# Attention products of stacked head pairs as four 64x64 tiles side by side

## The chip, the core and the metric

The kernel runs on one core of a Trainium2 chip. The metric is the device time of one execution in microseconds (us). A core has several engines that work side by side, each through its own instructions in order: TensorE (PE in the profile; PEld is its loading of weights), VectorE (DVE), ScalarE (ACT), GpSimd (POOL) and SyncE (SP). On this kernel POOL and SP also issue the DMA transfers. TensorE takes a stationary operand (the weights) and streams the columns of a second operand past it; the results go to PSUM, which has eight banks of 512 32-bit columns on 128 partitions.

## The reference

Two parts follow each other: an attention with a local and a pooled half, and a gated feed-forward network. The sizes are 8 batches, 8 heads, 576 positions, 64 channels a head; 4608 tokens of 512 channels, and 1536 hidden channels.

```python
q_d, k_d, v_d = (x.reshape(B, H, S // 4, 4, D).mean(axis=3) for x in (q, k, v))
out_up = np.repeat(sm_attn(q_d, k_d, v_d), 4, axis=2)      # softmax attention on 144 pooled positions
mask = np.abs(pos[:, None] - pos[None, :]) < 4             # local: keys at a distance of up to 3
scores = np.where(mask, scale * q @ k.T, -1e9)
attn = softmax(scores)
x = (out_up + attn @ v).transpose(0, 2, 1, 3).reshape(B * S, H * D)
out = (np.maximum(x @ w_gate, 0) * (x @ w_val)) @ w_out
```

## The kernel before

**The work and its order.** The 64 heads are worked on as 32 pairs, numbered from 0. Four pairs make one batch's share of the feed-forward input `xT`; the tokens then go through the feed-forward network in nine chunks of 512. The attention of later pairs is laid between the feed-forward work of earlier chunks. There is no loop that sets this order: the long string `SEQ` is a list of some 2,300 steps, emitted one after another, and every engine takes its own instructions in that order. A step such as `exp/a0/1@4` names the kind (`exp`), the pair within its chunk (`a` or `b`, and the half `1` of chunk `4`), and an argument (`0`). The kinds that matter here:

- `qk`, `v`, `v4`: DMA loads of a pair's Q and K, of its V, and of V for pooling. `qk` and `v` are issued by POOL, `v4` of the later pairs by SP. The step `scores` also issues the transposing DMA of the pair three further on, on SP.
- `pool` (DVE), `kk` and `kd` (ACT, L805 and L812), `scores` (PE, L842 and L846), `exp` (ACT, L855), `ed` (ACT, L860), `mask` (DVE, L868): from Q and K to the exponentials of the local and of the pooled scores.
- `o` (PE, L873, L888, L893): the denominators and numerators of the softmax.
- `ln` and `inv` (ACT, L905 and L923): one over the denominator, as Exp(-Ln(den)). `xn` (DVE, L908) multiplies, `xsum` (DVE, L912) adds the two halves into `xT`.
- `sq`, `up`, `p`, `q`, `qv` (PE, L1289, L1193, L1030): the 256-column products of the feed-forward network, which is computed in seven products for eight on 2x2 blocks; `sk`, `uk` (ACT, L1300) copy a quarter of a PSUM bank onto another so that PE adds to it; `sf`, `uf` (ACT, L1305, or DVE, L1307) give the finished quarters; `vh`, `hg`, `hv` (PE, L945) are plain 512-column products; `gt` (DVE, L1384) multiplies gate and value.

**The pairs that the change touches.** The pairs from 12 on (`NEW = 12`, 20 pairs) are stacked: the keys of head 0 stand on partitions 0 to 63 and those of head 1 on 64 to 127. A block of 58 queries sees 64 keys, so the local half is ten blocks; the pooled half is three sets of 48 keys. The weights of every product are 128x128 and block-diagonal, with zeros between the heads, and one matmul serves both heads. For one pair the step `o` comes in four parts, which `SEQ` places singly:

- `o/?00` (`emit_pooled`, L870, twice): three matmuls of 144 columns with a constant into the denominators, and three with the pooled V into the numerators;
- `o/?01`: the local denominators, two matmuls of 290 and 286 columns with `one_st`;
- `o/?10` and `o/?11`: the local numerators, five blocks of 58 columns each, with the block's V as weights.

The denominators lie in PSUM banks 4 and 5 and the numerators in 6 and 7, each as 576 local and 144 pooled columns, with head 0 on partitions 0 to 63. One `ln` over 128 partitions then reads all 720 denominators. The same banks hold scores and feed-forward quarters at other times.

**The earlier pairs** (below 12) are not stacked. They use two tiles of 64 weight columns beside each other, one for a head (L751, L760, L772, L781).

Of the kernel before, what the change touches and what calls it, by code (L numbers as in the profile page):

```python
# [11 lines left out]
AF = mybir.ActivationFunctionType  # L12
# [53 lines left out]
sq/4.0.0.1/0@2 hv/5/1@1 gate/5/1@1 xq/1/0@2 gate/4/1@1 xq/2/0@2 scores/a/0@2 sumhi/0/0@2 xq/3/0@2 v2/a/0@2 next/0/1@1
sumhi/1/0@2 next/1/1@1 sq/4.0.0.5/0@2 zero/k/1 kk/b1/0@2 vh/10.6/0@2 sk/4.0.0.1/0@2 sq/4.0.0.2/0@2 sq/4.0.0.6/0@2
exp/a0/0@2 sk/4.0.0.2/0@2 up/2.1/0@2 sq/4.0.0.7/0@2 sq/4.0.0.3/0@2 uk/2.1/0@2 sf/4.0.0.11/0@2 sk/4.0.0.5/0@2
vh/4.7/0@2 mask/a0/0@2 up/2.5/0@2 ed/a/0@2 kk/b0/0@2 sf/4.0.0.22/0@2 sq/4.0.0.4/0@2 up/2.6/0@2 sf/4.0.0.12/0@2
gt/4.7.0/0@2 sum/2/0@2 o/a00/0@2 sf/4.0.0.21/0@2 kd/b1/0@2 sq/0.0.2.1/0@2 sq/0.0.2.5/0@2 o/a01/0@2 o/a11/0@2  # L70
uk/2.2/0@2 uk/2.5/0@2 kd/b0/0@2 sk/0.0.2.1/0@2 sk/0.0.2.5/0@2 sum/3/0@2 up/2.7/0@2 zero/v/2 gt/10.6.1/0@2 next/0/0@2
v1/a/0@2 after/3/0@2 uf/2.22/0@2 ln/a0/0@2 inv/a/0@2 up/2.3/0@2 sq/0.0.2.6/0@2 o/a10/0@2 sq/0.0.2.2/0@2 sk/0.0.2.2/0@2
up/2.2/0@2 sq/0.0.2.3/0@2 sq/0.0.2.7/0@2 xn/a0/0@2 sf/0.0.2.11/0@2 uf/2.11/0@2 sf/0.0.2.22/0@2 sf/0.0.2.12/0@2
pool/a/0@2 up/2.4/0@2 uf/2.21/0@2 v2/b/0@2 uf/2.12/0@2 scores/b/0@2 exp/b0/0@2 v4/b/0@2 v1/b/0@2 sq/1.1.0.1/0@2
sq/1.1.0.5/0@2 sq/0.0.2.4/0@2 vh/0.7/0@2 sk/1.1.0.1/0@2 sk/1.1.0.5/0@2 ed/b/0@2 sf/0.0.2.21/0@2 sq/1.1.0.6/0@2
sq/1.1.0.2/0@2 vh/6.3/0@2 sk/1.1.0.2/0@2 sf/1.1.0.11/0@2 kk/a0/0@2 kd/a1/0@2 gt/0.7.2/0@2 sq/1.1.0.7/0@2
sq/1.1.0.3/0@2 vh/1.0/0@2 sf/1.1.0.22/0@2 sf/1.1.0.12/0@2 mask/b0/0@2 v4/a/0@2 kd/a0/0@2 kk/a1/0@2 sq/2.2.0.1/1@2
sq/1.1.0.4/0@2 sq/2.2.0.5/1@2 sf/1.1.0.21/0@2 gt/6.3.3/0@2 sk/2.2.0.1/1@2 o/b00/0@2 o/b01/0@2 gt/1.0.0/0@2 xsum/a/0@2
o/b10/0@2 o/b11/0@2 vh/7.1/0@2 next/2/0@2 gt/7.1.1/0@2 sq/2.2.0.6/1@2 up/0.1/1@2 ln/b0/0@2 inv/b/0@2 xn/b0/0@2
scores/a/1@2 sk/2.2.0.5/1@2 sk/2.2.0.2/1@2 uk/0.1/1@2 exp/a0/1@2 ed/a/1@2 kk/b1/1@2 sq/2.2.0.7/1@2 sq/2.2.0.2/1@2  # L80
sq/2.2.0.3/1@2 qk/a1/1@2 v1/a/1@2 up/0.5/1@2 sf/2.2.0.22/1@2 tm/b/0@2 sq/2.2.0.4/1@2 vh/8.7/1@2 qk/b3/1@2 v/a/1@2
next/1/0@2 v2/b/1@2 qk/a0/1@2 qk/a2/1@2 qk/a1/0@3 mask/a0/1@2 pool/b/1@2 sf/2.2.0.11/1@2 sf/2.2.0.21/1@2
sf/2.2.0.12/1@2 gt/8.7.1/1@2 up/0.6/1@2 kk/a0/1@2 sq/3.2.1.1/1@2 sq/3.2.1.5/1@2 kd/b0/1@2 uk/0.2/1@2 sk/3.2.1.1/1@2
vh/2.4/1@2 o/a10/1@2 uk/0.5/1@2 sq/3.2.1.6/1@2 sk/3.2.1.5/1@2 sk/3.2.1.2/1@2 qk/a3/1@2 gt/2.4.0/1@2 xsum/b/0@2
o/a00/1@2 up/0.7/1@2 kk/b0/1@2 sq/3.2.1.7/1@2 sf/3.2.1.22/1@2 next/3/0@2 uf/0.22/1@2 tm/a/1@2 kd/b1/1@2 v/b/1@2
pool/a/1@2 sq/3.2.1.2/1@2 o/a01/1@2 ln/a0/1@2 inv/a/1@2 sq/3.2.1.3/1@2 o/a11/1@2 sq/3.2.1.4/1@2 up/0.2/1@2
sf/3.2.1.21/1@2 scores/b/1@2 exp/b0/1@2 xn/a0/1@2 v/b/0@3 mask/b0/1@2 xsum/a/1@2 ed/b/1@2 up/0.4/1@2 uf/0.21/1@2
sf/3.2.1.11/1@2 up/0.3/1@2 sq/5.2.0.1/1@2 sq/5.2.0.5/1@2 o/b00/1@2 o/b01/1@2 vh/3.0/1@2 sk/5.2.0.1/1@2 uf/0.11/1@2
uf/0.12/1@2 kd/a0/1@2 sq/5.2.0.6/1@2 sf/3.2.1.12/1@2 gt/3.0.1/1@2 sk/5.2.0.2/1@2 o/b10/1@2 vh/9.1/1@2 gt/9.1.2/1@2
sk/5.2.0.5/1@2 ln/b0/1@2 sq/5.2.0.3/1@2 sq/5.2.0.2/1@2 sq/5.2.0.7/1@2 o/b11/1@2 v4/b/0@6 kd/a1/1@6 v2/b/1@6  # L90
sf/5.2.0.12/1@2 inv/b/1@2 sf/5.2.0.22/1@2 pool/a/1@6 v2/a/1@6 qk/b3/0@7 kd/a1/1@2 vh/5.4/1@2 sf/5.2.0.11/1@2
sq/5.2.0.4/1@2 sf/5.2.0.21/1@2 kk/a1/1@2 xn/b0/1@2 vh/11.1/1@2 gt/5.4.0/1@2 up/2.1/0@3 tm/b/1@2 v2/a/1@2 qk/b1/1@2
qk/b2/1@2 v1/b/1@2 qk/a0/0@3 qk/a2/0@3 v4/b/1@2 qk/b0/1@2 gt/11.1.1/1@2 qk/b3/0@3 qk/a3/0@3 qk/b0/0@3 v4/a/1@2
qk/b2/0@3 v/a/0@3 sq/4.0.0.1/0@3 kk/b0/0@3 sk/4.0.0.1/0@3 kk/b1/0@3 xsum/b/1@2 qk/b1/0@3 xq/0/0@3 xq/1/0@3 xq/2/0@3
scores/a/0@3 uk/2.1/0@3 vh/10.6/0@3 qk/b0/1@6 qk/a1/0@7 qk/a3/1@6 sq/4.0.0.2/0@3 sq/4.0.0.5/0@3 sq/4.0.0.6/0@3
sf/4.0.0.11/0@3 sumhi/0/0@3 xq/3/0@3 sk/4.0.0.5/0@3 sk/4.0.0.2/0@3 vh/4.7/0@3 v2/a/0@3 next/0/1@2 sumhi/1/0@3
next/1/1@2 sq/4.0.0.7/0@3 ed/a/0@3 exp/a0/0@3 kk/a1/0@3 sq/4.0.0.3/0@3 sf/4.0.0.22/0@3 up/2.5/0@3 sq/4.0.0.4/0@3
sf/4.0.0.21/0@3 up/2.6/0@3 uk/2.5/0@3 uk/2.2/0@3 sf/4.0.0.12/0@3 gt/4.7.0/0@3 o/a00/0@3 sq/0.0.2.1/0@3 sq/0.0.2.5/0@3
mask/a0/0@3 sum/2/0@3 sum/3/0@3 gt/10.6.1/0@3 pool/b/0@3 o/a01/0@3 o/a11/0@3 up/2.7/0@3 sk/0.0.2.1/0@3 sk/0.0.2.5/0@3
sq/0.0.2.6/0@3 sk/0.0.2.2/0@3 up/2.3/0@3 ln/a0/0@3 inv/a/0@3 kd/b1/0@3 sq/0.0.2.3/0@3 sq/0.0.2.2/0@3 sq/0.0.2.7/0@3  # L100
up/2.2/0@3 o/a10/0@3 uf/2.22/0@3 sf/0.0.2.12/0@3 uf/2.11/0@3 kd/b0/0@3 next/0/0@3 up/2.4/0@3 v1/a/0@3 after/3/0@3
sq/1.1.0.1/0@3 sf/0.0.2.22/0@3 xn/a0/0@3 sq/0.0.2.4/0@3 sk/1.1.0.1/0@3 uf/2.21/0@3 v2/b/0@3 uf/2.12/0@3 scores/b/0@3
# [207 lines left out]
def kernel(  # L310
# [559 lines left out]
    def emit_pooled(hp, lo, weights):  # L870
        for w in range(3):
            e = ep[hp % 2].rearrange("p (c t) -> p c t", c=2)
            nc.tensor.matmul(  # L873
# [744 lines left out]
```

## Time and profile before

| | |
|---|---|
| three runs | 334.12, 335.16, 335.21 us (median 335.16) |
| span of the profiled execution | 333.2 us, 9166 instructions |
| PE, DVE, ACT, POOL busy | 327.2, 288.9, 268.4, 185.2 us |
| granted TensorE clock | 1.000 |
| loads and stores | 43.96 MB by DMA |

The profile is of one execution. Its span runs from the program's first to its last instruction; the time of that same execution, which has some more around it, is not marked among the three. In rows of groups the columns are: line, engine, operation, out<-in by the program's names, shapes, count, then busy us and mean ns of one, then idle time before them and what ended it. A matmul's shape `128*128 128x256` means weights of 128 rows by 128 columns and 256 streamed columns. Durations of matmuls contain the time from the first column to the last result, so consecutive ones overlap in the list.

### The profile page before, as it was taken

How to read it: one execution, taken by the hardware profiler on the slowest of the kernel's cores; microseconds unless marked ns; L12 is line 12 of the kernel's file. 1: busy time of each engine (PE TensorE's matmuls, PEld its weight loads, DVE VectorE, ACT ScalarE, POOL GpSimd, SP SyncE). 2: the span in 40 equal slices, each digit the busy share in tenths (PEclk: the TensorE clock that was granted, in tenths of full speed). 3: DMA queues.
4: the chain of work that ended last, by engine and by line, in shares of the span. 5: the costliest groups of instructions: out<-in, count | busy, mean ns of one | idle time of the engine just before them, and what ended most of it. 6: DMA issues, size and time to landing. Idle time of an engine off the chain costs nothing.

```text
span 333.2 us, 9166 instructions
## 1 busy us (share of the span) xinstructions
PE 327.2 (98%) x3456; PEld 243.8 (73%) x3456; DVE 288.9 (87%) x574; ACT 268.4 (81%) x649; POOL 185.2 (56%) x268
## 2 busy tenths in 40 slices
PE   7999999999999999999999999999999999999996
PEld 3876556666577787778687868786878678888875
DVE  6795779999998989999999989979998998788792
ACT  4968887789988989899789989898889548787852
POOL 8974855938979889767968997855420000000000
PEclk9999999999999999999999999999999999999999
DMA  9999999999999999999999999999200102003014
GB/s 147 174 185 213 173 199 172 143 182 143 151 182 147 221 114 189 160 210 87 215 148 187 118 206 156 200 95 198 41 31 3 65 0 97 1 18 111 2 56 135
DMA packets 155264, 43.96 MB, mean 132 GB/s; under 512 B 140012, under 2 KB 149908, under 8 KB 155220
## 3 DMA queue, kind: packets, MB, share of 16 engines
q0 software_dynamic: 116800, 19.51, 82.6%
q1 hardware_dynamic: 38308, 23.83, 34.2%
q8 instruction: 27, 0.44, 0.6%
q14 instruction: 17, 0.14, 0.2%
q10 hardware_dynamic: 112, 0.04, 0.1%
HBM read 46.63 MB, written 9.44 MB: 168 GB/s over the span
## 4 chain that ended last, share of the span: by engine, by line
PE 91%; DMA 4%; POOL 1%; ACT 1%; DVE 1%; issue 1%; SPq 1%; POOLq 0%; ACTq 0%
PE ps L945 28%; PE ps L1289 26%; PE ps L1193 18%; PE ps L1030 3%; PE ps L873 2%; DMA v<-in_v_dram 2%; DMA qk<-in_q_dram 2%; PE ps L893 2%; PE ps L846 2%; PE ps L888 1%; PE ps L553 1%; PE ps L842 1%; PE ps L631 1%; PE ps L661 1%; PE ps L650 1%
## 5 line engine op out<-in xcount | busy, mean ns | idle before, releaser
L945 PE MATMUL ps<-xT,wv_sb 128*128 128x512 f16 x352 | 89.9, 379 | 0.0
L945 PEld LDWEIGHTS <-wv_sb 128*128 128x128 f16 x352 | 32.7, 98 | 26.0
L1384 DVE SCALAR_TENSOR_TENSOR gT<-r,ps 128x512 f16<-128x512 f16 x55 | 37.3, 681 | 4.8 <-PE ps L945 4.0
L1289 PE MATMUL ps<-xT,qk 128*128 128x256 f16 x240 | 41.3, 272 | 0.1
L472 POOL DMA_DIRECT2D qk<-in_q_dram x46 | 34.1, 741 | 10.6 <-DMA qkT<-qk 6.1
L472 POOL DMA_DIRECT2D qk<-in_k_dram x46 | 33.6, 733 | 11.4 <-issue 6.5
L1300 ACT COPY ps<-ps 128x256 f32<-128x256 f32 x80 | 28.6, 365 | 6.3 <-PE ps L1289 5.0
L1289 PE MATMUL ps<-xT,wg_sb 128*128 128x256 f16 x180 | 33.6, 272 | 0.0
L490 POOL DMA_DIRECT2D vw<-in_v_dram x40 | 28.9, 730 | 6.9 <-DMA qk<-in_q_dram 4.6
L540 DVE TENSOR_REDUCE qkd<-qkT 128x288 f16<-128x1152 f16 x23 | 30.8, 1340 | 0.0
L1204 ACT COPY ps<-ps 128x256 f32<-128x256 f32 x54 | 19.7, 370 | 12.7 <-PE ps L1193 11.4
L1289 PEld LDWEIGHTS <-qk 128*128 128x128 f16 x240 | 22.4, 97 | 7.6 <-issue 0.7
L610 POOL TENSOR_TENSOR vd<-v 48x192 f16<-48x192 f32 x40 | 25.7, 642 | 1.7
L945 PE MATMUL ps<-xT,wg_sb 128*128 128x512 f16 x104 | 26.6, 379 | 0.0
L1305 ACT CAST r<-ps 128x256 f16<-128x256 f32 x55 | 20.0, 372 | 7.5 <-PE ps L1289 6.6
L602 POOL TENSOR_TENSOR v<-v 112x384 f32<-112x384 f32 (+1 forms) x21 | 21.5, 1024 | 7.6 <-DMA v<-in_v_dram 7.3
L1289 PEld LDWEIGHTS <-xo 128*128 128x128 f16 x240 | 22.7, 98 | 3.4 <-DVE xo L1024 0.2
L1289 PE MATMUL ps<-wt,xo 128*128 128x256 f16 x180 | 24.4, 272 | 0.0
L923 ACT ACTIVATE rden<-rden 128x720 f32<-128x720 f32 x28 | 22.5, 804 | 0.7
L957 DVE TENSOR_TENSOR gT<-r,ps 128x512 f16<-128x512 f16 x24 | 16.2, 680 | 6.8 <-ACT r L954 4.0
L1289 PEld LDWEIGHTS <-wg_sb 128*128 128x128 f16 x180 | 16.4, 98 | 6.1 <-issue 0.2
L1307 DVE TENSOR_TENSOR r<-ps,xT 128x256 f16<-128x256 f32 x44 | 17.3, 418 | 3.4 <-PE ps L1289 2.4
(181 smaller groups left out, 876.3 us busy)
## 6 DMA issues: line engine op xcount, KB each, us to landing
out_dram<-y_sb SPq DMA_DIRECT2D x24, 256.0 KB, 4.2
v<-in_v_dram SPq DMA_DIRECT2D x20, 192.0 KB, 5.3
qk<-in_q_dram POOLq DMA_DIRECT2D x46, 72.0 KB, 6.1
qk<-in_k_dram POOLq DMA_DIRECT2D x46, 72.0 KB, 6.0
vw<-in_v_dram POOLq DMA_DIRECT2D x38, 80.0 KB, 5.1
v<-in_v_dram SPq DMA_DIRECT2D x20, 144.0 KB, 5.9
out_dram<-y_sb SPq DMA_DIRECT2D x22, 128.0 KB, 1.8
vw<-in_v_dram POOLq DMA_DIRECT2D x12, 168.0 KB, 6.9
```

Of the source, the lines that this page charges most:

```text
L472: nc.gpsimd.dma_start(dst.rearrange("p (j h d) -> p j h d", h=2, d=64)[:, :, hh, :], _dap(src, off + hh * S * D, [[D, 96], [NQ * D, NB], [ ...
L490: nc.gpsimd.dma_start(t[lo : lo + 64, j0:j1, lo : lo + 64], _dap(v, base + j0 * QB * D, [[D, 64], [QB * D, j1 - j0], [1, D]]),)
L540: nc.vector.tensor_reduce(out=qkd[hp % 2].rearrange("p i t -> p (i t)"), in_=qkT[hp % 4][:, 0 : 2 * S].rearrange("p (t f) -> p t f", f=4), ...
L602: nc.gpsimd.tensor_tensor(out=m, in0=t[:, :, 0:128], in1=t[:, :, 128:256], op=ALU.add)
L610: nc.gpsimd.tensor_tensor(out=vp[hp % 3][lo : lo + 48, :, lo : lo + 64], in0=m[:, :, 0:64], in1=m[:, :, 64:128], op=ALU.add)
L923: nc.scalar.activation(out=rden, in_=rden, func=AF.Exp, scale=-1.0)
L945: nc.tensor.matmul(out=out, lhsT=w[:, kk, bass.ts(jj, 128)], rhs=xT[:, kk, c * TCH : (c + 1) * TCH], start=(kk == 0), stop=(kk == 3),)
L1193: nc.tensor.matmul(out=out, lhsT=self.left[i][t], rhs=self.right[i][t], start=(i == 1 and t == 0), stop=(t == n - 1), skip_group_check=True,)
L1289: nc.tensor.matmul(out=out, lhsT=self.left[i - 1][k], rhs=self.right[i - 1][k], start=(i == 1 and k == 0), stop=(k == n - 1), skip_group_c ...
L1300: nc.scalar.copy(out=o, in_=x)
L1305: nc.scalar.copy(out=o, in_=self.d if i == 11 else self.a)
L1384: lambda c, jj, b, t: nc.vector.scalar_tensor_tensor(out=gT[c % 2][:, jj, :], in0=tg[t], scalar=0.0, in1=ps[:, b, :], op0=ALU.max, op1=ALU ...
```

## The change

The four parts of `o` of a stacked pair become one step, `emit_quads`. It uses only the diagonal quarters of the old weights. Each head has one stream of numerators (ten local blocks, three pooled matmuls) and one of denominators (two local, three pooled). Head 0 takes partitions 0 to 63 of the operands, and head 1 64 to 127. The numerators go to the head's own partitions, and the denominators to those of the other head, so that the four streams work on four different quarters of TensorE's array. Head 0 takes the local blocks first, and head 1 the pooled ones, then the blocks of the second bank and then those of the first. `emit_tiles` lists the matmuls of all four streams by a planned start (a step of 30 ns at least, else columns / 2.4 + 3; 4 ns between the streams).

Since the denominators stand on the other head's partitions, `ln` is split in two instructions of 64 partitions, which bring them back. `inv`, `xn` and `xsum` stay.

`SEQ` has a new order. It is the same for its first 457 steps; from there on it holds the same steps except for `o` (one for four) and `ln` (two for one), in other places: the loads `qk`, `v` and `v4` too.

```diff
+    def emit_tiles(streams):
+        steps = []
+        for n, stream in enumerate(streams):
+            t = 4.0 * n
+            for step in stream:
+                steps.append((t, n, step))
+                t += max(30, step[2].free_size() / 2.4 + 3)
+        for _, _, (out, left, right, first, last) in sorted(steps, key=lambda x: x[:2]):
+            nc.tensor.matmul(out=out, lhsT=left, rhs=right, start=first, stop=last, skip_group_check=True)
+
-    def emit_out_st(hp, i):
+    def emit_quads(hp):
         num, den = 512 * 6, 512 * 4
...
+        e, s, r = ep[hp % 2].rearrange("p (c t) -> p c t", c=2), es[hp % 2], hp % 3
+
+        streams = []
+        for h in range(2):
+            p, o = 64 * h, 64 - 64 * h
+            rows, some = slice(p, p + 64), slice(p, p + 48)
+            nums = [
+                (flat[rows, num + 222 + a : num + 222 + a + n], vb[hp % NL][rows, j, rows], s[rows, a : a + n], True, True)
+                for j, (a, n) in enumerate(blocks())
+            ]
+            dens = [
+                (flat[o : o + 64, den + 222 + a : den + 222 + b], one_st[rows, rows], s[rows, a:b], True, True)
+                for a, b in ((0, 290), (290, S))
             ]
+            pool = [
+                [
+                    (flat[t : t + 64, n + 798 : n + 942], left(w), e[some, :, SD:] if w == 2 else e[some, w, 0:SD],
+                     w == 0, w == 2)
+                    for w in range(3)
+                ]
+                for t, n, left in (
+                    (p, num, lambda w: vp[r][some, w, rows]),
+                    (o, den, lambda w: four_st[some, rows]),
                 )
+            ]
+            for a, b, k in ((nums, pool[0], 5), (dens, pool[1], 1)):
+                streams.append(a + b if h == 0 else b + a[k:] + a[:k])
+        emit_tiles(streams)
...
-    def emit_ln_st():
-        nc.scalar.activation(out=rden_st, in_=flat[:, 2048 + 222 : 2048 + 942], func=AF.Ln)
+    def emit_ln_st(h):
+        p, o = 64 * h, 64 - 64 * h
+        nc.scalar.activation(out=rden_st[p : p + 64], in_=flat[o : o + 64, 2048 + 222 : 2048 + 942], func=AF.Ln)
...
-        "o": lambda hp, a: emit_out_st(hp, 2 * int(a[0]) + int(a[1])),
-        "ln": lambda hp, a: emit_ln_st(),
+        "o": lambda hp, a: emit_quads(hp),
+        "ln": lambda hp, a: emit_ln_st(int(a)),
```

More of the change, by code (lines that the diff above doesn't have):

```diff
@@ L68 @@
[L68 to L72, printed above, removed]
@@ L98 @@
[L98 to L102, printed above, removed]
```

347 lines of the change are left out of this document (164 added, 183 removed).

## The prediction

> **What bounds the kernel now.** I read the page's busy shares and its chain of waits first, then a table of busy time by stage, then who waited for whom inside the stage that the change touches.
>
> ```profile
> span 333.2 us, 9166 instructions
> PE 327.2 (98%) x3456; PEld 243.8 (73%) x3456; DVE 288.9 (87%) x574; ACT 268.4 (81%) x649; POOL 185.2 (56%) x268
> PEclk9999999999999999999999999999999999999999
> PE 91%; DMA 4%; POOL 1%; ACT 1%; DVE 1%; issue 1%; SPq 1%; POOLq 0%; ACTq 0%
> ```
>
> PE is busy almost throughout at its full granted clock, and 91% of the chain is PE. The stacked pairs (the 20 pairs numbered 12 to 31) have their products between 98.5 and 264.5 us, so that is the stage to read. The table by stage gives busy us, and the count of instructions, of each engine:
>
> ```profile
> core 0: us, PE busy (x) PEld busy (x) DVE busy (x) ACT busy (x) POOL busy (x), PEclk, DMA share, GB/s
> 98.50:264.50 166.00, 165.60 (x1668) 127.38 (x1667) 153.19 (x277) 145.97 (x347) 113.47 (x169) 1.00 1.27 141
> 264.50:333.20 68.70, 65.48 (x573) 55.68 (x570) 54.08 (x122) 43.49 (x138) 0.00 (x0) 1.00 0.16 51
> 151.00:158.50 7.50, 7.50 (x92) 6.45 (x91) 7.01 (x13) 7.42 (x18) 5.20 (x10) 1.00 1.56 81
> 140.00:150.00 10.00, 10.00 (x96) 7.46 (x95) 9.33 (x15) 9.54 (x24) 7.06 (x11) 1.00 1.06 201
> ```
>
> In the 166.0 us of that stage PE works 165.6, DVE 153.2 and ACT 146.0. ACT idles 20.0 us. The lists of waits of this stage (us in total, times, longest) say why:
>
> ```profile
> ACT r L1305 <- PE ps L1289: 6.6, 12, 1.0
> ACT ps L1300 <- PE ps L1289: 4.7, 13, 0.8
> PE ps L873 <- POOL vd L610: 0.4, 1, 0.4
> ```
>
> ACT waits for PE; PE waits for nobody but once, 0.4 us. So PE sets the pace alone, and a PE microsecond saved is a microsecond gained only as long as ACT and DVE, at 88% and 92%, can follow.
>
> **Part 1: the products as 64x64 tiles.** A matmul's listed duration contains its latency, so I price one by the distance to the next start. PE's timeline (start, us, line, operands, count) around the products of pair 12 in the kernel before:
>
> ```profile
> 98.65 0.35 PE L873 MATMUL ps<-att 128*128 128x144 f16 x3
> 98.83 0.35 PE L873 MATMUL ps<-att,vd 128*128 128x144 f16 x3
> 99.02 0.38 PE L1289 MATMUL ps<-xT,wg_sb 128*128 128x256 f16 x2
> ...
> 99.46 0.41 PE L888 MATMUL ps<-att,one_st 128*128 128x290 f16 x2
> 99.71 0.30 PE L893 MATMUL ps<-att,vw 128*128 128x58 f16 x5
> 99.85 0.82 PE L1289 MATMUL ps<-wt,xo 128*128 128x256 f16 x6
> 100.50 0.71 PE L1289 MATMUL ps<-wo_sb,xo 128*128 128x256 f16 x5
> ```
>
> The six pooled products take 99.02 - 98.65 = 0.37 us (62 ns for 144 columns), the two denominators 99.71 - 99.46 = 0.25, five numerator blocks 99.85 - 99.71 = 0.14 to 0.15 (29 ns for 58 columns); the second five the same. A pair costs 0.37 + 0.25 + 0.29 = 0.91 us of PE. (Six products of 256 columns take 100.50 - 99.85 = 0.65, 109 ns each: the unit for all distances below.)
>
> The new step issues 36 products instead of 18, in four streams. The numerator streams are the longest: ten blocks of 58 columns and three of 144, 10 x 30 + 3 x 63 = 0.49 us; a denominator stream has 2 x 124 + 3 x 63 = 0.44. Four tiles at once do not occur in this trace; two do, in the pairs below 12, which put two heads side by side with 64 weight columns each:
>
> ```profile
> 29.76 1.03 PE L945 MATMUL ps<-xT,wg_sb 128*128 128x512 f16 x4
> 30.71 0.31 PE L751 MATMUL ps<-att,ones_sb 112*64 112x288 f16 x2
> 30.86 0.23 PE L760 MATMUL ps<-att,ones_sb 72*64 72x72 f16 x4
> ...
> 31.44 0.23 PE L781 MATMUL ps<-att,vd 72*64 72x72 f16 x4
> 31.61 0.45 PE L631 MATMUL ps<-vw,cst_sb 112*128 112x128 f16 x5
> ```
>
> Each head there streams 4 x 288 + 8 x 72 = 1728 columns; in single file two heads would be 3456 columns, 1.44 us at 2.4 columns a ns (above, 256 columns take 47 ns more than 144). The block lies between 30.71 and 31.51, 0.80 us: two streams cost the time of one. So I take the four streams as parallel, 0.50 us with the stagger of 4 ns. The same rows price the change of tile shape. The four 512-wide products before it start every 0.216 us from 29.76, so the next was due at 30.62 and started at 30.71: 0.09 lost. On the way out the last pair of tiles started at 31.48, was through by 31.51, and L631 started at 31.61: 0.10 lost. Each new step pays both: 0.50 + 0.19 = 0.69 us against 0.91, **0.22 us x 20 = 4.4 us less PE work**. The two ends: if the streams went two by two the step would be (2 x 0.49 + 2 x 0.44)/2 + 0.19 = 1.12 us, 4.2 us more in all; if the change of shape cost nothing, 0.50 us, 8.2 us less. The rows of two streams at full rate are the nearest, so I take 0.69.
>
> [...] No run here shows two row tiles in one bank: the trace's two-tile products are tiles of columns. [...]
>
> **Part 2: the logarithm in two halves.** The denominators land on the other head's partitions, so one ACTIVATE over 128 partitions becomes two over 64. What ACT pays depends on the elements, not the partitions (last columns: busy us, mean ns, idle before):
>
> ```profile
> L905 ACT ACTIVATE rden<-ps 128x720 f32<-128x720 f32 x20 | 15.4, 772 | 0.9 <-PE ps L888 0.7
> L855 ACT ACTIVATE att<-ps 128x576 f16<-128x576 f32 x20 | 13.1, 655 | 1.0 <-PE ps L846 0.5
> L805 ACT COPY kk<-qkT 64x640 f16<-64x640 f16 x20 | 14.5, 723 | 0.3
> L812 ACT COPY cst_sb<-qkd 64x144 f16<-64x144 f16 x40 | 12.4, 310 | 0.7
> ```
>
> On 64 partitions 496 more elements cost 723 - 310 = 413 ns, 0.83 ns each; on 128 partitions 144 more cost 117 ns, 0.81 each. A half logarithm of 720 elements is therefore as long as the whole one, 0.77 us. Consecutive instructions overlap a little: ACT's timeline shows a logarithm of 0.76 us whose successor starts 0.66 us later.
>
> ```profile
> 157.26 0.76 ACT L905 ACTIVATE rden<-ps 128x720 f32<-128x720 f32 x1
> 157.92 0.72 ACT L805 COPY att<-qkT 64x640 f16<-64x640 f16 x1
> ```
>
> So ACT gains 20 x 0.66 = 13.2 to 20 x 0.77 = 15.4 us in the stage: 145.97 becomes 159.2 to 161.4, middle 160.3. PE's 166.0 becomes 161.6. **ACT, which had 20 us to spare, has 0 to 2 left**; DVE keeps 153.2 of some 162, 95%. What hid ACT's lateness until now (its own waits for PE) is used up.
>
> **Part 3: the steps ordered anew.** The order is the same up to about 72 us, and after it holds the same steps but for the products and logarithms; so no other engine time is added. Three things move. (a) The four product steps of a pair become one, behind the mask, with both banks of each side free at once. PE issues in order, so a late mask (DVE, L868) or a late xn of the pair before (L908, which reads the numerator banks) now holds back all 36 products and every gate product behind them. Adding PE durations of the steps between mask and products gives -0.4 to 3.9 us before and 0.7 to 3.5 after: enough cover for a mask of 0.57, so nothing is booked. (b) Some loads of V move close to their use. Those of pairs 14, 30 and 31 stood 31, 40 and 37 us of PE work ahead of their products, and stand 6.4, 5.9 and 5.8 ahead now; behind other POOL work each takes two issues and a landing (first row: mean ns after the bar; second: us to landing):
>
> ```profile
> L490 POOL DMA_DIRECT2D vw<-in_v_dram x40 | 28.9, 730 | 6.9 <-DMA qk<-in_q_dram 4.6 <-DMA qk<-in_k_dram 1.1 <-issue 0.6
> vw<-in_v_dram POOLq DMA_DIRECT2D x38, 80.0 KB, 5.1
> ```
>
> 2 x 0.73 + 5.1 = 6.6 us, 0.2 to 0.8 us more than the cover: 0 to 2 us for the three, booked at 0 since the last two fall where the queues run empty, kept in the range. The loads of Q and K are put on POOL's queue at other places too, but the transposes that read them stay 24 to 28 us of PE work ahead of the scores. (c) ACT and PE loads now run level. Summed along the new order, with the distances above and ACT's means, from pair 12's Exp to the last pair's sum, ACT's total never departs from PE's by more than some 3 us, where before it fell behind steadily to 16 us.
>
> **The sum.** The stage needs 161.6 us for PE and about 160.3 for ACT, which feed each other all the time (PE fills a quarter of a bank, ACT copies it, PE adds to the copy). How full can ACT be while PE runs? The rows give both ends: 7.42 of 7.50 us (98.9%) in one stretch with PE at 100%, and 9.54 of 10 (95.4%) in the fullest 10 us stretch that I looked at. I take 98%, nearer the first, because in both rows ACT was waiting for PE, which will no longer be so: 160.3/0.98 = 163.6 us, 2.4 us less than 166.0. The rest (98.5 and 68.7 us) has the same work. The span becomes 333.2 - 2.4 = **330.8 us**. The three runs' median of 335.16 lies 2.0 above the profiled span; I keep that: **332.8 us, 0.7% faster**, 2.0 us short of what PE alone would gain.
>
> **The rivals.** (A) ACT is hidden entirely: the stage is PE's 161.6, the span 328.8, the time 330.8. For it: 7.5 us with both engines full. Against it: one such stretch is not 160 us. (B) Slower: ACT becomes the bound and PE waits for its copies. With 95.4% the stage is 160.3/0.954 = 168.0, the span 335.2, the time 337.2; it turns slower than before once ACT is under 160.3/166.0 = 96.6% full. For it: no 10 us row above that. (C) The tiles don't run four abreast. If heads sharing bank 7 for 0.2 us take turns, a step is 0.89 us, PE's gain is 20 x 0.02 = 0.4, and the time 334.8, no change; two by two it is 335.16 + 4.2 = 339.4. Against it: two streams cost one. [...] (D) V comes late: up to 2 us on the forecast, 334.8 at worst.
>
> **How the numbers follow.** Forecast 0.42, A 0.15, B 0.22, C 0.12, D 0.09. About 0.5% (1.7 us: below 333.5, above 336.8) is what a measurement of this kernel can tell from no change. The forecast's own spread (97 to 99% full) is 331.1 to 334.5: 0.30 faster, 0.12 same. A is faster. B: 0.18 slower, 0.04 same. C: 0.07 same, 0.05 slower. D: 0.07 same, 0.02 faster. Faster 0.47, same 0.30, slower 0.23. The range runs from just under A to just over B, 330.2 to 338.0, and leaves the two-by-two case of C out.
>
> **What would show it.** Right: product groups of 36 that take 0.5 us with about 0.1 us lost on each side; 40 logarithms of about 0.77 us; ACT 157 to 161 us busy in the stage, its waits on PE nearly gone, and a few us of new PE waits for ACT (L1300 or L1305). Wrong: a product step of 0.9 us or more (C); PE waiting for vw or the DMAs of V (D); PE waits for ACT of over 5 us in sum (B); or half logarithms much shorter than 0.77 us, which would take away the reason for the 2 us loss.

## The result: 3.2% slower

The changed kernel takes 346.25 us (median of 4 runs, 343.75 to 346.87) against 335.07 for the kernel before on the same chip: 1.032 times as long, 95% interval 1.028 to 1.036. The forecast was 332.8, with a range of 330.2 to 338.0. The profiled execution took 346.87 us, its span is 345.1. Its page:

```profile
span 345.1 us, 9897 instructions
PE 330.3 (96%) x3816; PEld 238.2 (69%) x3816; DVE 292.1 (85%) x574; ACT 283.5 (82%) x669; POOL 187.0 (54%) x268
PEclk9999999999999989999999999999999999999999
PE 60%; ACT 12%; DMA 10%; POOL 6%; DVE 5%; issue 5%; SPq 0%; POOLq 0%; ACTq 0%; DVEq 0%
```

PE's share of the chain fell from 91% to 60%, and one slice has a lower clock (0.51 from 120.5 to 124.0 us). To place the loss, the same cuts by stage as before; the end of the stage is set by the last pair's sum into `xT`, which moved from 265.2 to 276.2 us:

```profile
core 0: us, PE busy (x) PEld busy (x) DVE busy (x) ACT busy (x) POOL busy (x), PEclk, DMA share, GB/s
0.00:98.50 98.50, 95.56 (x1219) 60.60 (x1220) 82.34 (x179) 78.17 (x165) 67.53 (x93) 1.00 1.74 173
98.50:275.50 177.00, 168.87 (x2026) 121.64 (x2025) 156.88 (x277) 161.32 (x366) 119.46 (x176) 0.99 1.22 132
```

The stage of the stacked pairs grew from 166.0 to 177.0 us, and that is nearly all of the 11.9 us by which the spans differ. In it ACT works 161.3 us and DVE 156.9: ACT is 91.1% full, DVE 88.6%, and no engine is at its limit by its own count. What changed is PE, which now waits (us in total, times, longest):

```profile
PE ps L874 <- DMA vw<-in_v_dram: 3.0, 1, 3.0
PE ps L1296 <- DVE r L1314: 2.0, 2, 1.3
PE ps L1296 <- ACT ps L1307: 0.5, 2, 0.3
PE ps L874 <- DVE att L864: 0.3, 1, 0.3
```

This list hides the short waits: a 256-column matmul is listed with some 0.27 us and the next one is due after 0.109, so a wait of under 0.2 us leaves no gap in it. Measured from start to start, as the prediction prices a matmul (whatever lies beyond the time due after the one ahead, and beyond the 0.09 us of a change of tile shape), PE lost 0.9 us in the stage before and 14.9 now: 5.7 waiting for ACT (34 times, 31 of them for the copies and casts of L1307 and L1312 and the logarithms of L912), 5.0 for DVE, 3.0 for one load of V, and 1.1 put down to nobody, in the stretch of the lower clock. PE's own work of 166.0 - 0.9 - 3.8 = 161.3 us (the 3.8 is worked out below) and the 14.9 make 176.2, all but 0.8 us of the measured 177.0.

### The profile page after: what moved, and what is told of

Read it like the earlier page. It is cut to its first block, busy times and chain, and to the rows that moved or that the text cites. A ratio compares the mean times of both kernels' runs of the same rounds, so it can differ in the third digit from the quotient of the medians.

```text
span 345.1 us, 9897 instructions
## 1 busy us (share of the span) xinstructions
PE 330.3 (96%) x3816; PEld 238.2 (69%) x3816; DVE 292.1 (85%) x574; ACT 283.5 (82%) x669; POOL 187.0 (54%) x268
## 4 chain that ended last, share of the span: by engine, by line
PE 60%; ACT 12%; DMA 10%; POOL 6%; DVE 5%; issue 5%; SPq 0%; POOLq 0%; ACTq 0%; DVEq 0%
PE ps L1200 17%; PE ps L952 16%; PE ps L1296 15%; DMA v<-in_v_dram 4%; ACT rden L912 3%; POOL qk L468 3%; DMA qkT<-qk 2%; PE ps L874 2%; DMA vw<-in_v_dram 2%; ACT ps L1307 2%; DMA qk<-in_k_dram 2%; PE ps L1037 1%; POOL v L598 1%; PE ps L549 1%; ACT r L1312 1%
## 5 line engine op out<-in xcount | busy, mean ns | idle before, releaser
L952 PEld LDWEIGHTS <-wv_sb 128*128 128x128 f16 x352 | 33.4, 98 | 27.0 <-issue 0.7
L1296 PE MATMUL ps<-xT,qk 128*128 128x256 f16 x240 | 41.9, 275 | 1.3 <-DVE xT L1283 0.4
L1391 DVE SCALAR_TENSOR_TENSOR gT<-r,ps 128x512 f16<-128x512 f16 x55 | 36.4, 680 | 4.3 <-PE ps L952 3.3
L1296 PE MATMUL ps<-xT,wg_sb 128*128 128x256 f16 x180 | 33.4, 272 | 2.6 <-DVE r L1314 2.0
L912 ACT ACTIVATE rden<-ps 64x720 f32<-64x720 f32 x40 | 30.6, 765 | 4.6 <-PE ps L874 3.8
L1307 ACT COPY ps<-ps 128x256 f32<-128x256 f32 x80 | 28.7, 366 | 3.3 <-DVE gT L1391 1.2
L1296 PEld LDWEIGHTS <-qk 128*128 128x128 f16 x240 | 22.5, 98 | 11.8 <-issue 3.3
L598 POOL TENSOR_TENSOR v<-v 112x384 f32<-112x384 f32 (+1 forms) x21 | 22.0, 1056 | 13.2 <-DMA v<-in_v_dram 12.9
L1211 ACT COPY ps<-ps 128x256 f32<-128x256 f32 x54 | 19.7, 370 | 11.6 <-PE ps L1200 10.2
L606 POOL TENSOR_TENSOR vd<-v 48x192 f16<-48x192 f32 x40 | 26.7, 666 | 1.7
L1314 DVE TENSOR_TENSOR r<-ps,xT 128x256 f16<-128x256 f32 x44 | 18.3, 419 | 9.2 <-PE ps L1296 7.5
L1312 ACT CAST r<-ps 128x256 f16<-128x256 f32 x55 | 20.0, 373 | 6.7 <-PE ps L1296 6.1
L1296 PEld LDWEIGHTS <-xo 128*128 128x128 f16 x240 | 22.9, 98 | 3.4 <-DVE xo L1031 0.2
L1296 PEld LDWEIGHTS <-wg_sb 128*128 128x128 f16 x180 | 16.8, 97 | 12.1 <-issue 4.7
L1296 PE MATMUL ps<-wt,xo 128*128 128x256 f16 x180 | 24.3, 273 | 0.1
```

Source lines behind the costliest of these rows:

```text
L598: nc.gpsimd.tensor_tensor(out=m, in0=t[:, :, 0:128], in1=t[:, :, 128:256], op=ALU.add)
L606: nc.gpsimd.tensor_tensor(out=vp[hp % 3][lo : lo + 48, :, lo : lo + 64], in0=m[:, :, 0:64], in1=m[:, :, 64:128], op=ALU.add)
L912: nc.scalar.activation(out=rden_st[p : p + 64], in_=flat[o : o + 64, 2048 + 222 : 2048 + 942], func=AF.Ln)
L952: nc.tensor.matmul(out=out, lhsT=w[:, kk, bass.ts(jj, 128)], rhs=xT[:, kk, c * TCH : (c + 1) * TCH], start=(kk == 0), stop=(kk == 3),)
L1296: nc.tensor.matmul(out=out, lhsT=self.left[i - 1][k], rhs=self.right[i - 1][k], start=(i == 1 and k == 0), stop=(k == n - 1), skip_group_c ...
L1307: nc.scalar.copy(out=o, in_=x)
```

## The experiments

**Theories.** A, the capacity of ACT: it has less to spare than its idle time says, and its 15 us more of logarithms are the loss, wherever they stand. P, the place: the second half logarithm stands between the denominators and the Exp, and holds banks that PE wants. O, the order: the steps placed anew cost by themselves. L: the one late load of V is the cause. (These letters are not those of the prediction's rivals.) Each ratio below is against the kernel before, timed on the same chip in the same series, with its 95% interval. Edits are shown shortened. Line numbers shift by a few lines between the runs: L1296, L1290, L1285, L1293 and L1298 are the same 256-column products.

**e1, V of pair 14 loaded before pair 12's products.** In the list of steps:

```
- ln/b1/0@2 sk/2.2.0.5/1@2 up/0.1/1@2 v/a/1@1 gt/7.1.1/0@2
+ ln/b1/0@2 sk/2.2.0.5/1@2 up/0.1/1@2 gt/7.1.1/0@2
- next/0/0@2 zero/v/2 o/a00/0@2
+ next/0/0@2 zero/v/2 v/a/1@1 o/a00/0@2
```

> The changed kernel with one step moved: the load of V of pair 14 stands before the products of pair 12, some 13 us earlier. Theory L (late loads): the wait of 3.1 us before pair 14's products, the slow clock after it (3.4 us at half speed, 1.7 us lost) and 0.4 us within these products go, 346.25 becomes 341 to 342. Theory A (a full ScalarE sets the pace): ScalarE was not idle for the whole of that wait, so the time is found again as waits for ScalarE further on, 344 to 346.

Measured: 345.40 us, 1.030 (1.024 to 1.035), span 344.7. PE's waits:

```profile
PE ps L1296 <- DVE r L1314: 3.0, 4, 1.3
PE ps L874 <- POOL vd L606: 1.4, 1, 1.4
PE ps L952 <- DVE y_sb L1314: 1.2, 1, 1.2
```

The wait for V and the lower clock are gone (a mean of 1.000 in its profile), and the median is 0.9 us lower, which the intervals don't tell from nothing. Others took its place: 1.4 us for the sums of V at the same product step, and more for DVE. The late load is real but not the cause.

**e3, one half logarithm.**

```
     def emit_ln_st(h):
+        if h == 1:
+            return
```

> The changed kernel without the second half logarithm of each stacked pair (one head's denominators are not refreshed): ScalarE has some 13 to 15 us less work, everything else stands. Theory A: the waits of PE for ScalarE (5.8 us in sum in the changed kernel) and most of those for VectorE (5.0 us) go, 336 to 339, and the late V of pair 14 stays. Theory O: little changes, 343 to 346.

Measured: 340.42 us, 1.016 (1.010 to 1.023), between what the two theories wanted. The second half logarithm costs 5.8 us, half of the loss. The other half is not ACT's amount of work: that is back to 269.9 us in the span, against 268.4 in the kernel before.

**e4, the new order alone,** with the old products as one block and one logarithm:

```
- "o": lambda hp, a: emit_quads(hp),
+ "o": lambda hp, a: [emit_out_st(hp, i) for i in range(4)],
- "ln": lambda hp, a: emit_ln_st(int(a)),
+ "ln": lambda hp, a: emit_ln_st() if <the later of the two ln steps> else None,
```

> The new order with the old products, all four steps of a pair at the place of the new one, and the one logarithm at the place of the second half. PE has 4.4 us more work than in the changed kernel, ScalarE 13 to 15 us less. Theory O: the waits stay and the PE work is added, 347 to 351. Theory A: the waits go but for the late V of pair 14, 338 to 341.

Measured: 342.83 us (four runs, 340.65 to 345.97), 1.025 (1.017 to 1.033): the order alone costs 7.6 us by the medians, between what A and O wanted. Against e3 (the same order, also one logarithm) the new products save 2.4 us by the medians, but the intervals overlap, so this saving isn't shown. Where the order loses, PE waits for DVE:

```profile
PE ps L1285 <- DVE r L1303: 1.7, 3, 0.8
PE ps L1285 <- DVE xT L1272: 0.7, 1, 0.7
```

**e2, e5, e7, e8: the new products in the old order.** The old order has four places for the products of a pair and the new step needs all its banks at once, so there is no neutral place for it. In e2 I put it at the last of the four (which for one of the pairs is behind the next pair's scores in the same banks, and overwrites them in part); in e5 earlier, behind the last gate product in the list that uses one of its banks. e7 is e5 with one logarithm over all 128 partitions (each head is then divided by the other's denominators), e8 is e5 with the copies of the pooled keys moved from ACT to GpSimd:

```
e7: -            p, o = 64 * h, 64 - 64 * h
    -            nc.scalar.activation(out=rden_st[p : p + 64], in_=flat[o : o + 64, ...], func=AF.Ln)
    +            if h == 0:
    +                nc.scalar.activation(out=rden_st, in_=flat[:, 2048 + 222 : 2048 + 942], func=AF.Ln)
e8: (emit_kd) -  nc.scalar.copy(
              +  nc.gpsimd.tensor_copy(
```

> The order of steps of the kernel before, with the new products at the place of the last of the four old product steps, and the two half logarithms at the place of the one. Theory O (the new order is at fault): the time is that of the kernel before less up to 4.4 us of PE, 331 to 334. Theory A: ScalarE has 13 to 15 us more work in any order, PE waits for it, 338 to 344.

> The order of the kernel before, with the new products where the last part of the old denominators stood (behind the last gate product that still reads the numerators' banks) and the two half logarithms where the one stood, so that no step on the shared banks changes its place against them. Theory O (the new order alone is at fault): 335.2 less the 4.4 us of PE, 331 to 332. Theory A (a full ScalarE makes PE wait in any order): 336 to 342.

> The same as e5_old_order with one logarithm of 128 partitions, which leaves each head with the other head's denominators. The products' part alone: PE has 4.4 us less, ScalarE as before. Both theories: 331 to 332 if no other engine holds PE back; above 333 would mean that VectorE (92% busy) or the placing behind the mask does.

> The same as e5_old_order with the 40 copies of pooled keys (64x144, 0.31 us each on ScalarE) made by GpSimd, which idles 50 us in the stage: ScalarE has 11 to 12 us less than in e5_old_order. Theory A: most of what e5_old_order loses comes back, 331 to 334. Theory O: the same time as e5_old_order. If the copies hold up GpSimd's queue of loads, the time is above that of e5_old_order.

Measured: e2 379.44 us (1.130), e5 358.73 (1.068, 1.061 to 1.074), e7 345.58 (1.029, 1.024 to 1.035), e8 362.82 (1.083, 1.078 to 1.088). None of them is the test I meant. In e2 the products come right before the logarithms, and PE waits 12.0 us for these and 14.5 for ACT's copies and casts. e7, which has no work added to any engine, shows what the placement of e5 costs: PE waits at the product step until DVE has read the gate product that still holds its banks.

```profile
PE ps L875 <- DVE gT L1392: 5.5, 3, 2.8
```

What can be read is the difference of e5 and e7, 13.2 us for the second half logarithm in that order, and that GpSimd is no place for the copies there: in e8 PE waits 7.5 us for them, in five places.

**e6, the kernel before with its logarithm in two halves,** the clean test of part 2:

```
-        nc.scalar.activation(out=rden_st, in_=flat[:, 2048 + 222 : 2048 + 942], func=AF.Ln)
+        for p in (0, 64):
+            nc.scalar.activation(out=rden_st[p : p + 64], in_=flat[p : p + 64, 2048 + 222 : 2048 + 942], func=AF.Ln)
```

> The kernel before with its logarithm split in two instructions of 64 partitions, each on its own partitions; nothing else changes. ScalarE has 13 to 15 us more, PE the same. Theory A: PE waits for ScalarE, 337 to 343. Theory O: the 20 us that ScalarE had idle take it up, 335 to 336.

Measured: 346.63 us, 1.033 (1.030 to 1.036). Twenty more logarithms and nothing else cost 10.9 us, as much as the whole change. PE, which waited for nobody but once before, now waits for ACT:

```profile
PE ps L1290 <- ACT ps L1301: 3.9, 7, 0.9
PE ps L842 <- ACT rden L906: 1.6, 6, 0.4
```

Both A and P fit this: the waits are for the copies of the feed-forward quarters, but also for the logarithms themselves.

**e10 and e11, the same amount of ACT work where nobody waits for it.** To tell A from P, copies of zeros into unused memory, two a pair (e10) or one (e11), in the kernel before:

```
     def emit_xsum_st(hp):
+        nc.scalar.copy(out=junk, in_=zero_sb[0:64, 0:256])
+        nc.scalar.copy(out=junk, in_=zero_sb[0:64, 0:256])   # e10 only
```

> The kernel before, with two more ScalarE copies of 64x256 half precision per stacked pair, at the step that adds up x; they read zeros and write memory that nothing reads in this stage. Nobody waits for them and they hold no PSUM bank. From 0.19 us plus 0.81 ns an element they should take 0.40 us each, 14 to 16 us for the 20 pairs: the dose that the second half logarithms add. Theory of capacity (any ScalarE work added costs most of its length, since ScalarE and TensorE run in lock step and ScalarE's idle time is no reserve): 344 to 347 us, as much as the split logarithm alone (346.6). Theory of the chain (the half logarithm costs because it stands between the denominators and the Exp and holds the banks of the next gate products): the copies lie in ScalarE's idle time, 335 to 338 us. Between them, 339 to 343, both have a share.

> The same with one copy per stacked pair, 7 to 8 us of ScalarE work. Capacity: half the loss, 339.5 to 342. Chain: 335 to 336.5. If ScalarE has a reserve that is used up somewhere between, this one costs nothing (335 to 336) and the full dose of two copies costs 4 us or more.

Measured: e10 343.66 us, 1.023 (1.019 to 1.028), just under what the theory of capacity wanted; e11 336.30, 1.0035 (1.001 to 1.006). The first dose is nearly free and the second costs 7.4 us, almost its length. The engine rows of e11, e10 and e6, in this order, give the amounts (ACT's busy time in the span, with overlaps counted once; the row of the kernel before stands in the prediction, 268.4):

```profile
PE 328.4 (98%) x3456; PEld 243.8 (73%) x3456; DVE 288.9 (86%) x574; ACT 273.6 (82%) x669; POOL 187.5 (56%) x268
```

```profile
PE 329.9 (97%) x3456; PEld 243.9 (71%) x3456; DVE 290.0 (85%) x574; ACT 281.1 (82%) x689; POOL 185.8 (54%) x268
```

```profile
PE 332.1 (96%) x3456; PEld 244.3 (71%) x3456; DVE 289.1 (84%) x574; ACT 283.8 (82%) x669; POOL 185.6 (54%) x268
```

| | ACT work added, us | time added, us | difference |
|---|---|---|---|
| e11 | 273.6 - 268.4 = 5.2 | 336.30 - 335.44 = 0.9 | 4.3 |
| e10 | 281.1 - 268.4 = 12.7 | 343.66 - 335.44 = 8.2 | 4.5 |
| e6 | 283.8 - 268.4 = 15.4 | 346.63 - 335.75 = 10.9 | 4.5 |
| the change | 283.5 - 268.4 = 15.1 | 346.25 - 335.07 = 11.2 | 3.9 |

By this count about 4.4 us of ACT work are free and each further microsecond costs about one. The copies of e10, which nobody waits for, lie on the same line as the logarithms of e6, which stand in the chain. So most of the loss goes with the amount (8.2 us without any place in the chain, against 10.9), and P can't be the whole of it. P isn't ruled out for the rest. By the instructions' own durations, in which overlaps count twice, e10 adds 20 x (0.405 + 0.403) = 16.2 us and e6 only 30.6 - 15.4 = 15.2, and yet e6 costs 2.7 us more; by that count the free part is not 4.4 us but 4 to 8. The copies of e10, then the logarithms of e6 (the 15.4 are in the prediction):

```profile
L915 ACT COPY vw<-zero_sb 64x256 f16<-64x256 f16 x20 | 8.1, 405 | 0.6
L914 ACT COPY vw<-zero_sb 64x256 f16<-64x256 f16 x20 | 8.1, 403 | 0.2
```

```profile
L906 ACT ACTIVATE rden<-ps 64x720 f32<-64x720 f32 x40 | 30.6, 766 | 0.7 <-PE ps L888 0.2
```

By either count the 20 us that ACT idled were no reserve of 20 us; with 4.4 more ACT is (146.0 + 4.4)/166.0 = 90.6% full. In e10 (its stage, then ACT's waits, then PE's) ACT still waits for PE while PE waits for ACT:

```profile
98.50:272.50 174.00, 168.24 (x1662) 127.07 (x1660) 153.83 (x276) 158.02 (x385) 112.74 (x168) 1.00 1.13 134
```

```profile
ACT r L1309 <- PE ps L1293: 5.6, 10, 1.3
ACT ps L1304 <- PE ps L1293: 3.2, 11, 0.7
```

```profile
PE ps L1293 <- ACT ps L1304: 3.2, 7, 0.6
```

In the kernel before ACT's two rows were 6.6 and 4.7 us. With 12.7 us more to do ACT waits only 2.5 us less for PE in them. I read it so: the two pass quarters of a bank to and fro, and a step that ends late on one side starts late on the other.

**e9, the changed kernel with less to do for ACT:** the copies of pooled keys left out from pair 14 on.

```
     def emit_kd(hp, hh):
+        if hp >= NEW + 2:
+            return
```

> The changed kernel without the ScalarE copies of the shared key blocks (64x144, two per pair) from pair 14 on; the scores of those pairs are taken with the keys of pairs 12 and 13. That takes 18 x 2 x 0.31 = 11 us of work from ScalarE, at a place that has nothing to do with the logarithm. Theory of capacity: most of the 5.8 us that the second half logarithm costs comes back, and more, 338 to 341 us. Theory of the chain: these copies are early, nobody waits for them, 344 to 346 as the changed kernel (346.25).

Measured: 341.80 us, 1.017 (1.012 to 1.022): 4.4 us came back for some 10 of ACT work (283.5 to 273.4 us in the span). By the table, 5.0 us more than the kernel before should cost 0.6; it costs 6.4. So the table does not hold in the new order, and something other than ACT's amount of work keeps the time at 340 to 342 us, where e3 also stands. PE waits there for DVE:

```profile
PE ps L1298 <- DVE r L1316: 3.1, 3, 1.3
```

**What makes DVE late.** The longest of these waits in the changed kernel, by the timelines of PE, DVE and POOL:

```profile
200.11 1.03 PE L952 MATMUL ps<-xT,wv_sb 128*128 128x512 f16 x4
202.40 0.38 PE L1296 MATMUL ps<-xT,wg_sb 128*128 128x256 f16 x2 [1.26 <-DVE r L1314]
```

```profile
199.93 2.08 DVE L919 TENSOR_TENSOR xT<-xn 128x576 f16<-128x576 f16 x1
201.93 0.74 DVE L1314 TENSOR_TENSOR r<-ps,xT 128x256 f16<-128x256 f32 x2
```

```profile
199.61 0.75 POOL L468 DMA_DIRECT2D qk<-in_k_dram  x1
200.37 1.01 POOL L598 TENSOR_TENSOR v<-v 112x384 f32<-112x384 f32 x1
```

The sum into `xT` (L919), 0.75 us at the median, takes 2.08: it starts while GpSimd issues a load, 0.44 us before GpSimd adds a pair's V, and ends 0.63 us after that addition. The addition that PE waits for (L1314) is queued behind it. Summed over DVE instructions that took over 0.15 us more than the median of their form, from 90 us on, it is 5.0 us before, 6.7 after and 8.5 in e4.

**e12 and e13, without GpSimd's sums of V from pair 15 on,** in the new order alone (e12) and, as its control, in the kernel before (e13):

```
-        if NVP <= hp < NP:          (emit_v2; in emit_v1 likewise)
+        if NVP <= hp < min(NP, 15):
```

> The kernel with the new order alone (products as one block, old tiles, one logarithm: 342.8 us), without GpSimd's sums of V from pair 15 on; the pooled part of those pairs uses old sums. If the order costs 7.6 us because VectorE's steps, now closer together, are stretched beside GpSimd's additions and the issues of loads that wait behind them: 337 to 340. If the order's cost is the waits of TensorE for the reciprocal and the mask, with GpSimd no part of it: 341.5 to 343.5.

> The kernel before, without GpSimd's sums of V from pair 15 on (the pooled part of those pairs uses old sums): the control of the same edit in the new order, which gave 4.7 us. If the old order hides the stretched VectorE steps (TensorE lost only 0.9 us in its stage): 334.5 to 335.5, no change. If the sums cost any order as much: 330 to 331.5, and the new order has no part in it.

Measured: e12 338.16 us, 1.009 (1.006 to 1.013), 4.7 less than e4; e13 334.05, 0.996 (0.995 to 0.998), 1.3 less than its kernel before. The same edit is worth 1.3 us in the old order and 4.7 in the new. The sum into `xT` is back to its length (the row of e4, then that of e12), and the stretch in all fell from 8.5 to 1.7 us:

```profile
L908 DVE TENSOR_TENSOR xT<-xn 128x576 f16<-128x576 f16 x20 | 16.5, 823 | 0.1
```

```profile
L908 DVE TENSOR_TENSOR xT<-xn 128x576 f16<-128x576 f16 x20 | 15.0, 751 | 0.1
```

So by the medians some 3.4 of the 7.6 us of the order go with DVE beside GpSimd (e4's interval alone is 5 us wide); the stretch was there before, but cost only 1.3 us. (The edit also takes GpSimd's additions out of the way of its loads, which these runs don't separate.) The other 4.1 us (338.16 - 334.05) remain.

**e15, e14, e17, e16: the causes taken away together.** The changed kernel without those sums (e15), also with one half logarithm (e14), and both again with V of pair 14 early as in e1 (e17 and e16); the edits are the ones above.

> The changed kernel without GpSimd's sums of V from pair 15 on. If the order's cost (VectorE beside GpSimd) and the second half logarithm's (ScalarE) are two causes that add: 346.25 - 4.7 = 341 to 342. If one hides the other, ScalarE being the bound whatever VectorE does: 344 to 346.

> The changed kernel with only the first half logarithm (one head's numerators are divided by what the buffer still holds) and without GpSimd's sums of V from pair 15 on. If the costs add: 340.4 - 4.7 = 335 to 336.5. If these two are all that held the new order back, the 4.4 us of TensorE time come out and it is faster than the kernel before: 331 to 333.5. If neither: 338 or more.

> The same with both half logarithms, that is the changed kernel without GpSimd's sums from pair 15 on and with V of pair 14 early. The second half logarithm by itself, with the other two causes gone: 5 to 8 us above the run without it (e10's full dose cost 8.2), so 337 to 341. If late V and logarithm hide each other, as taking V's wait away gave only 0.9 us in the changed kernel: 340.5 to 341.5, as without the early V.

> As the changed kernel with the first half logarithm alone and without GpSimd's sums of V from pair 15 on, and with V of pair 14 loaded before pair 12's products. If the three causes (second half logarithm, VectorE beside GpSimd, one late V) are the whole loss, the TensorE time saved comes out: 331 to 333 (the kernel before without the sums takes 334.05, less 1 to 3). If something else in the new order costs as much as the new products save: 334 to 336. If the wait for V only hid another: 337 or more.

| V early | both half logarithms | one half logarithm |
|---|---|---|
| no | e15 341.31 (ratio 1.016 to 1.021) | e14 338.65 (1.005 to 1.012; 335.8 to 340.6) |
| yes | e17 340.97 (1.011 to 1.023) | e16 336.75 (1.003 to 1.005) |

Without GpSimd's sums the changed kernel is 4.9 us faster, as much as the order alone was. ACT is then fuller in its stage, 160.75/171.0 = 94.0%, so what an engine reaches depends on how late the others are, and 90.6% is no fixed limit. (The logarithms alone without GpSimd's sums were not run, so how far the two go together in the old order is open.)

```profile
98.50:269.50 171.00, 166.66 (x2026) 120.86 (x2024) 151.66 (x277) 160.75 (x365) 77.98 (x124) 1.00 1.28 137
```

The second half logarithm still costs 4.2 us (e17 to e16). The scatter of e14 goes with the load of V, which in its profile PE waits for as in the changed kernel: four of its nine runs, at full clock (1.000), take 335.8 to 338.6, the five below it (0.989 to 0.995) 338.65 to 340.6. Single effects on the changed kernel, 5.8 (logarithm), 4.9 (sums) and 0.9 (V), make 11.6; taken together they give 346.25 - 336.75 = 9.5. They may partly hide each other; the difference lies within the intervals. e15 fell where two causes that add would put it, and e16 above what three causes that are the whole loss would give.

Even e16 is 1.3 us slower than the kernel before, and 2.7 slower than e13, although its PE has 3.8 us less to do. PE still loses 4.6 us there by the distances of starts; the largest single wait is

```profile
PE ps L954 <- DVE y_sb L1316: 1.7, 1, 1.7
```

What sets the rest of the order's cost, some 4 us in this wait and many small ones, stays open. None of these versions with the new products or the new order beats the kernel before.

## Why the prediction was wrong

**Part 1, the products: right in kind, 0.03 us off.** PE's timeline around one of the twenty steps in the changed kernel:

```profile
192.41 0.82 PE L1296 MATMUL ps<-wt,xo 128*128 128x256 f16 x6
193.16 0.21 PE L874 MATMUL ps<-att,vw 64*64 64x58 f16 x1
193.17 0.31 PE L874 MATMUL ps<-att,one_st 64*64 64x290 f16 x1
193.17 0.25 PE L874 MATMUL ps<-att,vd 48*64 48x144 f16 x1
...
193.41 0.22 PE L874 MATMUL ps<-att,vw 64*64 64x58 f16 x3
193.44 0.22 PE L874 MATMUL ps<-att 48*64 48x144 f16 x1
193.44 0.22 PE L874 MATMUL ps<-att,vw 64*64 64x58 f16 x3
...
193.63 0.22 PE L874 MATMUL ps<-att,vw 64*64 64x58 f16 x2
193.79 0.61 PE L1296 MATMUL ps<-xT,qk 128*128 128x256 f16 x4
```

The first product was due at 192.41 + 6 x 0.109 = 193.06 and came at 193.16; the last started 0.50 us later, and the next shape at 193.79. That is 0.72 us a step against 0.69 foreseen, a saving of 20 x 0.19 = 3.8 us instead of 4.4, for a step that waits for nothing. In 18 of the 20 steps the 36 products took 0.50 us from first start to last. Rival C falls: the two heads' numerators, in bank 7 on different partitions around 193.42 (both `vw` rows), run beside each other. So do their second denominators, both in bank 5, which the prediction had not counted: they start 0.07 us apart (193.31 and 193.38) and stream 286 columns each, 0.12 us at 2.4 a ns, the rate of the prediction's 47 ns for 112 columns more. The 0.2 us for which rival C had the heads share bank 7 was an estimate from the plan of the streams: head 0 is due there from 5 x 0.03 = 0.15 us of the step on, head 1 until 3 x 0.063 + 5 x 0.03 = 0.34. No run shows them taking turns: the step that would then have taken 0.89 us took 0.72.

**Part 2, the logarithm in halves: right.** Forty of 0.765 us, and ACT at 161.3 us in the stage, where 159.2 to 161.4 was foreseen:

```profile
L912 ACT ACTIVATE rden<-ps 64x720 f32<-64x720 f32 x40 | 30.6, 765 | 4.6 <-PE ps L874 3.8
```

**Part 3: (a) and (c) wrong, (b) later than foreseen and yet priced within its bound.** (a) booked the order at 0 on the cover before the mask. e4 shows 7.6 us, and the waits are mostly not at the mask but for DVE's feed-forward additions (L1314 of the changed kernel, L1303 in e4). I had checked PE's cover of one step, and not whether DVE, at 92%, could keep up beside GpSimd in the new order; some 3.4 us of it hang on that. (b) V of pair 14 came 3.0 us late, where 0 to 2 was foreseen, those of pairs 30 and 31 did not matter, and taking the wait away gained 0.9 at most by the medians. (c) "level loads", that ACT's and PE's totals stay within 3 us of each other, says nothing of the waits, since each needs the other's result at every step.

**The sum: the steps that failed.** The first is the term "I take 98%" for how full ACT is over the whole stage: 91.1% was measured. e6, with the logarithms alone, has 161.49 of 177.50 us, 91.0%; with this in place of 98% the sum would give 160.3/0.910 = 176.2 us, within 0.8 of the 177.0 measured. (That is a fit made afterwards.) The second is the order, booked at 0 in part 3: it costs 7.6 us by itself (e4), so the forecast would have missed even with ACT at 98%.

The two rows that the 98% came from, 98.9% in 7.5 us and 95.4% in 10, were among the fullest stretches of a stage that had 88% as a whole. The changed kernel has such stretches too, twice as long:

```profile
120.00:140.00 20.00, 19.06 (x225) 13.76 (x228) 15.00 (x30) 17.05 (x37) 18.76 (x28) 0.91 1.54 153
140.00:160.00 20.00, 19.56 (x260) 14.52 (x249) 18.00 (x31) 19.50 (x45) 11.55 (x17) 1.00 1.65 152
180.00:200.00 20.00, 19.82 (x259) 14.35 (x258) 17.57 (x31) 19.60 (x48) 15.53 (x24) 1.00 1.28 155
200.00:220.00 20.00, 17.41 (x177) 12.13 (x175) 19.45 (x34) 15.84 (x38) 15.44 (x21) 1.00 1.30 144
```

From 140 to 160 and from 180 to 200 us ACT is 97.5% and 98.0% full, and it falls to 85.3% and 79.2% in the other two: until 121.6 us it waits 3.3 us for the products that the late V holds up, and from 200 to 220 us 3.8 us for DVE and for PE, which waits for DVE's late sums there. So 91.1% is a mean of nearly full stretches and of holes that others make, and not a level at which ACT runs: that the changed kernel lies near the line of the table doesn't show that it has the limit of e6. The reason given for the 98%, that ACT was waiting for PE in both rows, was a misreading: from 151.0 to 158.5 us the trace lists 0.3 us of such waits. In the changed kernel ACT's waits for PE's quarters did shrink as foreseen (the rows of 6.6 and 4.7 us to 3.9 and 0.9), and 3.8 us of waits for the new products came instead. Rival B had ACT's part right, with its turning point named (96.6%): PE waits 5.7 us for ACT, but also 5.0 for DVE and 3.0 for V. Its 337.2 was too low because it took its 95.4% from such a stretch too, and left the order out.

**What is shown and what isn't.** Shown: the second half logarithms alone, in the old order, cost as much as the whole change (e6), and most of that goes with the amount of ACT work (e10, e11); the new order costs time of its own (e4, and e3 and e9, which stay at 340 to 342 us with little ACT work added), part of it with GpSimd's sums beside DVE (e12 against e13). Either alone gives 340 us or more, so PE's 3.8 us could not come out. Open: how much the place of the logarithms adds (up to 2.7 us in e6 against e10), and the remaining 4 us of the order.

## What to carry to other kernels

An engine's idle time in a stage where it passes work to and fro with the bounding engine need not be a reserve; price its spare time by adding work that nobody waits for (here, by busy time, 4.4 of 20 us were free, and then each microsecond cost about one), not from the fullest stretch of the trace. A change that saves on the bounding engine by adding four times as much to the next one is to be judged on that one first. And when steps are ordered anew, look at which instructions of DVE and GpSimd then meet, for their durations are not constants (0.75 us became 2.08 here).

## What the runs showed of the hardware

- One of DVE's additions between SBUF operands was stretched beside GpSimd's work: 0.75 us became 2.08, ending 0.63 us after GpSimd's addition of 1.01 us. Without those additions the 20 sums of e12 average 751 ns instead of 823 in e4. The sum had begun 0.44 us before the addition, and no row shows what held it up. The 44 additions of DVE from PSUM and `xT` into `r` (L1314) were not stretched: they took 407 to 426 ns each.
- After its wait of 3.0 us PE ran at half its clock for 3.4 us, in the changed kernel's profile (the granted clock is the third number from the end). The two rows are the 3.5 us from the end of that wait on, and the next 3.5:

```profile
120.50:124.00 3.50, 3.50 (x48) 2.75 (x49) 0.52 (x2) 2.30 (x4) 2.77 (x4) 0.51 1.69 139
124.00:127.50 3.50, 3.50 (x73) 3.03 (x71) 2.67 (x5) 2.78 (x8) 3.24 (x5) 1.00 1.14 104
```

  Three of the four runs of the changed kernel have a mean clock of 0.995 (345.9 to 346.9 us), which 3.4 us at half speed would give; the fourth has 1.000 (343.75). The profile of e14 has 0.995 as well, that of e1, without the wait for V, 1.000, and that of e16, whose longest wait was 1.7 us, 0.998.
- A change of tile shape cost 0.09 to 0.10 us each way for 64x64 tiles too (0.72 us a step, of which 0.50 from first start to last and some 0.03 for the last product), and four streams of them cost the time of the longest (0.50 us).
